# Probabilities turned as halves of 64 queries, and a new order of the pairs' work, in a fused attention and mixture-of-experts kernel

## The chip, the cores and the metric

One core of one Trainium2 chip runs the whole kernel. The metric is device time in microseconds. The core's engines run each its own program in order and meet through semaphores: PE (TensorE, matmuls; PEld are its loads of the stationary operand), DVE (VectorE), ACT (ScalarE), POOL (GpSimd) and SP, which issues the transfers.

## What is computed

Attention over 8 batches, 8 heads, 576 positions and 64 dimensions, with a causal mask by blocks of 64; then a top-1 mixture of 8 experts, where each expert keeps at most 80 tokens.

```python
scores = scale * np.matmul(q, k.transpose(0, 1, 3, 2))
mask = block_i >= block_j                      # blocks of 64
scores = np.where(mask, scores, -1000000000.0)
attn = np.exp(scores - np.max(scores, axis=-1, keepdims=True))
attn = attn / (np.sum(attn, axis=-1, keepdims=True) + 1e-09)
x = np.matmul(attn, v)                         # then tokens x 512
...
expert_idx = np.argmax(x @ w_gate, axis=1)     # 80 tokens kept for each expert
h = np.maximum(x[tok_idx] @ w1[e], 0.0)
out[tok_idx] = gate_w[tok_idx, None] * (h @ w2[e])
```

## The kernel before

Attention goes by pairs: two heads of one batch, 32 pairs in all, four to a batch. The 576 queries of a pair are five groups: u = 0 to 3 with 128 queries for each head, and group 4, the last 64 queries of both heads together (head 0 in partitions 0 to 63, head 1 in 64 to 127). Group u sees 128(u+1) keys.

For each group: `scores` multiplies q and k into PSUM (`sc`, two buffers of two banks; the two heads lie in the upper and lower 64 rows of the array and write to a bank each), with a small matmul of `mneg` and `mrow` that masks; `max` on DVE takes the negated row maximum; `soft` on ACT writes the exponentials to the probability tiles `P` in SBUF and sums them. Groups 2 and 0 share one score buffer ("20"). The probabilities then have queries on partitions, and the product with v needs keys there, so `back` turns them on PE, block by block, against the identity, into PSUM tiles `pm` (four buffers of one bank, line 252), and `take` copies each full bank to the SBUF tile `PT`: on ACT ("a") or DVE ("v") as `TAKE` says. `values` multiplies with v: half 0 is the 512 queries of groups 0 to 3, half 1 the 64 of group 4. `flip` on DVE turns the result into rows of tokens.

`TURN` is the order of one iteration, written by hand: an entry is a pair's offset from the iteration's number and what is done for that pair. The loop (line 552) walks it once an iteration, and every engine gets its instructions in the order in which the entries stand. So iteration i does scores and exponentials of pair i, the blocks of group 4 and `values` of pair i-1, loads (`load`, `load_v`) for later pairs and their turning on DVE (`prep`; POOL scales the queries). Three entries "step" an iteration take the next piece of a finished batch from a list: sums, store, logits, gate and so on, nine pieces for a batch, so three of four iterations have such steps, and one, called quiet here, has none. After the pairs follow the choice of tokens and the experts.

Before the change `back` knows seven kinds, each into one bank: "30" and "31" (group 3 of each head, four blocks of 128x128), "1", "2", "20" (group 0's block and group 2's last one, both heads), "4" (four blocks of group 4) and "44" (its fifth block, padded to 128 keys). That is 25 transpositions for a pair. "44" shares its bank with `values` half 1.

Of the kernel before, what the change touches and what calls it, by code (L numbers as in the profile page):

```python
# [7 lines left out]
F32 = mybir.dt.float32  # L8
# [10 lines left out]
P = 128  # L19
BLK = 64  # L20
NT = 5
# [3 lines left out]
CHUNK = 80  # L25


TAKE = {"back": {"30": "v", "31": "a", "1": "a", "2": "a", "20": "a", "4": "v", "44": "a"}, "values": {0: "a", 1: "a"}}

GROUPS = {"3": ((3, 0),), "20": ((2, 0), (0, 384)), "1": ((1, 0),)}  # L30

TURN = (
    (3, "load"),
    (2, "load_v"),
    (0, "begin"),
    (0, "scores", "3"),
    (0, "scores", "20"),
    (0, "max", "3"),
    (-1, "back", "44"),
    (-1, "back", "4"),  # L40
    (-1, "take", "back", "44"),
    (0, "max", "20"),
    (-1, "take", "back", "4"),
    (-1, "values", 0),
    (0, "soft", 3, 1),
    (0, "soft", 3, 0),
    (0, "soft", 2, 0),
    (0, "soft", 2, 1),
    (-1, "values", 1),
    (1, "prep", 1),  # L50
    (0, "soft", 0, 1),
    (0, "step"),
    (0, "soft", 0, 0),
    (-1, "take", "values", 1),
    (-1, "take", "values", 0),
    (0, "scores", "1"),
    (0, "max", "1"),
    (0, "step"),
    (0, "soft", 1, 0),
    (0, "soft", 1, 1),  # L60
    (0, "back", "30"),
    (0, "back", "31"),
    (1, "prep", 0),
    (0, "take", "back", "30"),
    (0, "scores_4"),
    (0, "max_4"),
    (0, "step"),
    (0, "back", "20"),
    (0, "back", "2"),
    (0, "take", "back", "31"),  # L70
    (-2, "flip"),
    (0, "back", "1"),
    (0, "soft_4"),
    (0, "take", "back", "1"),
    (0, "take", "back", "20"),
    (0, "take", "back", "2"),
)


# [1 line left out]
def tile_attn_moe(ctx, tc, q, k, v, w_gate, w1, w2, capacity, out, xs=None, dbg=None):  # L81
    nc = tc.nc
    B, H, S, D = q.shape
    NTOK, DM = out.shape
    E, _, F = w1.shape
# [24 lines left out]
    big = att2.enter_context(tc.tile_pool(name="big", bufs=2))  # L110
# [13 lines left out]
    for i in range(4):  # L124
        r = slice(32 * i, 32 * i + 32)
# [112 lines left out]
                    mybir.DependencyClass.Sync, mybir.DependencyReason.DATA))  # L238


    Pt = []
    for i in range(2):
        row = [pb.tile([P, 2, P * (t + 1)], F32, name=f"P{i}_{t}") for t in range(NT - 1)]
        Pt.append(row + [pb.tile([P, P * NT], F32, name=f"P{i}_4")])

    VT = [pb.tile([P, 2, D], F32, name=f"vt{i}") for i in range(4)]

# [125 lines left out]
    class Pair:  # L373


        def __init__(self, i):
            self.i = i
            self.b, self.pr = divmod(i, NP)
            self.h0 = 2 * self.pr
            self.out = {}  # L380
            self.T = {}

        def load(self):

            b, h0 = self.b, self.h0
            self.nat = [ld.tile([P, S // 32, 32], F32, name=f"ld{x}") for x in range(2)]
            for x in range(2):
                for h in range(2):
                    for i in range(2):
                        r = slice(h * D + 32 * i, h * D + 32 * i + 32)  # L390
                        nc.sync.dma_start(self.nat[x][r], (q, k)[x][b, h0 + h, :, 32 * i:32 * i + 32]
                                          .rearrange("(g r) d -> r g d", r=32))
# [68 lines left out]
        def back(self, x):  # L461


            if x == "30":
                self.PT = big.tile([P, 2, 13, P], F32, name="PT")
            PT = self.PT
            row = Pt[self.i % 2]
            pt = ps_m.tile([P, 512], F32, name="pm")
            if x in ("30", "31"):
                h = int(x[1])  # L470
                blocks = [(3, h, j) for j in range(4)]
                dst = PT[:, h, 3:13:3]
            elif x in ("1", "2"):
                u = int(x)
                blocks = [(u, h, j) for h in range(2) for j in range(2)]
                dst = PT[:, :, u:u + 4:3]
            elif x == "20":
                blocks = [b for h in range(2) for b in ((0, h, 0), (2, h, 2))]
                dst = PT[:, :, 0:9:8]
            else:  # L480
                blocks = [(4, None, j) for j in (range(4) if x == "4" else (4,))]
                dst = PT[:, :, 10:12] if x == "4" else PT[:, 0, 7]
            for n_, (u, h, j) in enumerate(blocks):
                src = row[u] if h is None else row[u][:, h]
                nc.tensor.transpose(pt[:, P * n_:P * (n_ + 1)], src[:, P * j:P * (j + 1)], ident)  # L485
            src = pt[:, 0:P * len(blocks)]
            if len(dst.shape) == 3:
                src = src.rearrange("p (j c) -> p j c", c=P)
            elif len(dst.shape) == 4:
                src = src.rearrange("p (h j c) -> p h j c", h=2, c=P)  # L490
            self.out["back", x] = (dst, src)
            if x == "44":
                self.shared = pt

        def values(self, half):

            av = ps_m.tile([P, 512], F32, name="pm") if half == 0 else self.shared[:, P:2 * P]
            PT = self.PT
            for j in range(4 + half):
                for h in range(2):  # L500
                    lhs = self.vt[:, h, :] if j == 4 else self.vn[:, h, j, :]
                    if half == 0:
                        rhs, c0, end = PT[:, h].rearrange("p b c -> p (b c)")[:, 512 * j:512 + 384 * j], P * j, 512
                    else:
                        b = PT[:, 0, 7] if j == 4 else PT[:, j // 2, 10 + j % 2]
                        rhs, c0, end = b[:, h * BLK:(h + 1) * BLK], 0, BLK
                    nc.tensor.matmul(av[h * D:(h + 1) * D, c0:end], lhsT=lhs, rhs=rhs,  # L507
                                     start=(j == 0), stop=(j == 3 + half))
            self.out["values", half] = ((self.bt.xT[:, self.pr, 0:512], av) if half == 0 else
                                        (self.bt.xT[:, self.pr, 512:S], av[:, 0:BLK]))  # L510

        def flip(self):
            self.bt.flip(self.pr)
# [1 line left out]
        def take(self, what, x):  # L515

            if TAKE[what][x] == "a":
                nc.scalar.copy(*self.out.pop((what, x)))  # L518
# [14 lines left out]
    n = B * NP  # L533
    pairs = [Pair(i) for i in range(n)]

    for row in Pt:
        nc.gpsimd.memset(row[4][:, S:], 0.0)
    for t_ in VT:
        nc.gpsimd.memset(t_[BLK:P], 0.0)
    nc.gpsimd.memset(wgd, 0.0)  # L540
# [57 lines left out]
    ps_m = ctx.enter_context(tc.tile_pool(name="ps_m2", bufs=3, **ps))  # L598
# [43 lines left out]
    for h in (1, 0):  # L642
        pl = pall[h]
        for k in range(2):
            for g in range(2):
# [3 lines left out]
                                          rhs=spread[:, k, g].rearrange("p j i -> p (j i)"),  # L649
                                          start=(k == 0 and g == 0), stop=(k == 1 and g == 1))  # L650
# [241 lines left out]
    with tc.For_i(0, again, 1):  # L892
# [24 lines left out]
        step = 1.0  # L917
        for it in range(28):
# [12 lines left out]
                         start=True, stop=True)  # L931
# [54 lines left out]
        with tc.For_i(0, more, 1):  # L986
# [24 lines left out]
            for e in range(E):  # L1011
# [67 lines left out]
```

## Time and profile before

| | us |
|---|---|
| median of 3 runs | 481.56 (481.30 to 481.87) |
| the profiled execution | 480.64 |
| its span | 478.4 |
| attention, from the first maximum to the choice of tokens | about 11 to 355 |
| experts, the rest of the span | about 123 |

The page gives busy time of each engine as a share of the whole span, so attention and experts are mixed in it. The groups by line show what one instruction takes (mean, ns) and what ended the idle time ahead of it. The order of time shows starts, and from start to next start is what a run of work really holds its engine: matmuls overlap, and a matmul's recorded length holds its way through the array too. Line 485 is the transpositions, 423, 430 and 439 the scores, 507 the values, 518 and 520 the copies of `take` on ACT and DVE, 444 and 448 the maxima, 452 and 457 the exponentials. These are the groups of the transpositions' PE side and of the value matmuls:

```profile
L485 PE MATMUL pm<-ident,P 128*128 128x128 f32 x800 | 108.7, 280 | 0.3 <-ACT P L457 0.2
L485 PEld LDWEIGHTS pm<-ident,P 128*128 128x128 f32 x800 | 87.1, 141 | 21.8 <-issue 15.9
L507 PE MATMUL pm<-PT,vn 128*64 128x64 f32 (+4 forms) x1024 | 91.1, 330 | 1.4 <-DVE PT L520 1.0
```

In such a row, 128*128 are the rows and columns of the stationary operand (here the probabilities) and 128x128 the moving one (here the identity).

### The profile page before, as it was taken

Reading aid. Unit: us, or ns where it says so; the run is one execution under the profiler, and the core shown is the slowest. Engines: PE = TensorE matmul, PEld = TensorE weight load, DVE = VectorE, ACT = ScalarE, POOL = GpSimd, SP = SyncE. Lnnn points to the kernel's source line nnn. Section 1 sums busy time; section 2 is a strip of 40 time slices with the busy share of each in tenths; the row PEclk is TensorE's granted clock in tenths of the full one; section 3 lists DMA queues with packets and bytes.
Section 4 is the critical chain, followed back from the end, with each engine's and each line's share of the span. In section 5 each row is a group of like instructions: output and inputs, shape, how many; then the busy total and the mean of one; then the engine's idle time right before and its main releaser. Section 6 shows DMA issues by size and latency. Waiting matters only on the chain. (4 is left out here: it accounts for less than half of the span.)

```text
span 478.4 us, 13557 instructions
## 1 busy us (share of the span) xinstructions
PE 442.0 (92%) x5403; PEld 309.5 (65%) x5403; DVE 283.9 (59%) x564; ACT 272.7 (57%) x863; POOL 54.0 (11%) x112
## 2 busy tenths in 40 slices
PE   5999999999999999999999999999984897889992
PEld 3566656666666666666666666666563887778981
DVE  3657767787696778769677876977672311011111
ACT  1787777787778778777877877787611110011100
POOL 1002120010010001001000100100024400000010
PEclk9799999999999999999999999999997699999997
DMA  7677746897887688887878877843259999995001
GB/s 120 115 138 143 163 84 118 175 272 141 173 172 149 123 184 241 152 180 150 168 138 182 226 138 157 174 108 77 70 107 336 308 395 398 394 394 215 18 19 30
DMA packets 230676, 84.29 MB, mean 176 GB/s; under 512 B 196877, under 2 KB 215309, under 8 KB 230608
## 3 DMA queue, kind: packets, MB, share of 16 engines
q1 hardware_dynamic: 229584, 80.93, 69.3%
q0 software_dynamic: 1024, 2.43, 1.7%
q8 instruction: 44, 0.72, 0.6%
q14 instruction: 24, 0.20, 0.1%
HBM read 63.21 MB, written 20.33 MB: 175 GB/s over the span
## 5 line engine op out<-in xcount | busy, mean ns | idle before, releaser
L452 ACT ACTIVATE P<-sc,negm 128x512 f32<-128x512 f32 (+3 forms) x256 | 132.2, 536 | 29.9 <-DVE negm L444 29.8
L444 DVE TENSOR_REDUCE negm<-sc 128x2 f32<-128x1024 f32 (+3 forms) x128 | 99.6, 820 | 73.9 <-PE sc L430 73.9
L485 PE MATMUL pm<-ident,P 128*128 128x128 f32 x800 | 108.7, 280 | 0.3 <-ACT P L457 0.2
L485 PEld LDWEIGHTS pm<-ident,P 128*128 128x128 f32 x800 | 87.1, 141 | 21.8 <-issue 15.9
L423 PE MATMUL sc<-T,T 64*128 64x128 f32 (+3 forms) x512 | 91.2, 471 | 3.5 <-POOL T L408 2.5
L507 PE MATMUL pm<-PT,vn 128*64 128x64 f32 (+4 forms) x1024 | 91.1, 330 | 1.4 <-DVE PT L520 1.0
L518 ACT COPY PT<-pm 128x512 f32<-128x512 f32 (+1 forms) x160 | 77.1, 530 | 23.2 <-PE pm L485 22.6
L507 PEld LDWEIGHTS pm<-PT,vn 128*64 128x64 f32 x1024 | 52.1, 137 | 41.4 <-issue 29.7
L423 PEld LDWEIGHTS sc<-T,T 64*128 64x128 f32 x512 | 41.9, 188 | 32.7 <-ACT PT L518 10.2
L452 ACT ACTIVATION_READ_ACCUMULATOR P<-sc,negm 128x1 f32 x256 | 54.4, 212 | 0.0
L405 DVE STREAM_TRANSPOSE T<-ld 128x576 f32<-128x576 f32 x64 | 49.1, 768 | 4.1 <-DMA ld<-in_k_dram 4.1
L408 POOL TENSOR_SCALAR T<-T 128x576 f32<-128x576 f32 x32 | 21.5, 673 | 246.6 <-DVE T L405 181.6
L824 PE MATMUL ps<-xsT,w 128*64 128x80 f32 x1024 | 41.6, 243 | 4.2 <-issue 4.2
L824 PEld LDWEIGHTS ps<-xsT,w 128*64 128x64 f32 x1024 | 39.4, 144 | 5.6 <-issue 5.0
L520 DVE COPY PT<-pm 128x512 f32<-128x512 f32 x64 | 42.7, 667 | 0.5 <-PE pm L485 0.5
L824 PE MATMUL av<-hT,w 128*64 128x80 f32 x1024 | 38.2, 234 | 4.4 <-issue 4.4
L824 PEld LDWEIGHTS av<-hT,w 128*64 128x64 f32 x1024 | 36.4, 137 | 6.3 <-issue 6.3
L439 PE MATMUL sc<-T,T 64*64 64x288 f32 x256 | 38.5, 419 | 0.0
L457 ACT ACTIVATE P<-sc,negm 128x576 f32<-128x576 f32 x32 | 23.8, 745 | 20.3 <-DVE negm L448 20.3
L844 ACT ACTIVATE hT<-ps 128x320 f32<-128x320 f32 x16 | 7.0, 437 | 49.1 <-PE ps L824 49.1
L448 DVE TENSOR_REDUCE negm<-sc 128x1 f32<-128x576 f32 x32 | 24.3, 758 | 8.6 <-PE sc L439 7.8
L852 DVE COPY yT<-av 128x320 f32<-128x320 f32 x8 | 3.9, 492 | 38.1 <-PE av L824 38.1
(158 smaller groups left out, 303.2 us busy)
## 6 DMA issues: line engine op xcount, KB each, us to landing
w<-in_moe_w_dram SPq DMA_DIRECT2D x16, 2048.0 KB, 20.3
ld<-in_q_dram SPq DMA_DIRECT2D x128, 72.0 KB, 3.0
ld<-in_k_dram SPq DMA_DIRECT2D x128, 72.0 KB, 2.7
out_dram<-zero SPq DMA_DIRECT2D x18, 512.0 KB, 4.6
xs<-Y SPq DMA_DIRECT2D x32, 288.0 KB, 4.4
vn<-in_v_dram SPq DMA_DIRECT2D x64, 128.0 KB, 2.8
vt<-in_v_dram SPq DMA_DIRECT2D x32, 32.0 KB, 2.4
xs<-rs SPq DMA_DIRECT2D x8, 16.0 KB, 2.4
```

Source lines behind the costliest of these rows:

```text
L405: nc.vector.transpose(t, self.nat[x].rearrange("p g d -> p (g d)"))
L423: nc.tensor.matmul(s[:, h, c:c + P * (u + 1)], lhsT=self.T[0][r, P * u:P * (u + 1)], rhs=self.T[1][r, 0:P * (u + 1)], start=(x == 0), stop ...
L439: nc.tensor.matmul(s[r, c, 0:288], lhsT=self.T[0][r, 512:S], rhs=self.T[1][r, 288 * c:288 * (c + 1)], start=True, stop=True)
L444: nc.vector.tensor_reduce(self.negm[:, u], self.s[g][:, :, c:c + P * (u + 1)], axis=AX.X, op=ALU.max, negate=True)
L448: nc.vector.tensor_reduce(self.negm[:, 4, 0:1], self.s["4"][:, :, 0:288], axis=AX.XY, op=ALU.max, negate=True)
L452: nc.scalar.activation(Pt[self.i % 2][u][:, h], self.s[g][:, h, c:c + P * (u + 1)], AF.Exp, bias=self.negm[:, u, h:h + 1], scale=1.0, accu ...
L457: nc.scalar.activation(Pt[self.i % 2][4][:, 0:S].rearrange("p (c k) -> p c k", c=2), self.s["4"][:, :, 0:288], AF.Exp, bias=self.negm[:, 4 ...
L485: nc.tensor.transpose(pt[:, P * n_:P * (n_ + 1)], src[:, P * j:P * (j + 1)], ident)
L507: nc.tensor.matmul(av[h * D:(h + 1) * D, c0:end], lhsT=lhs, rhs=rhs, start=(j == 0), stop=(j == 3 + half))
L518: nc.scalar.copy(*self.out.pop((what, x)))
L520: nc.vector.tensor_copy(*self.out.pop((what, x)))
L824: yield nc.tensor.matmul(dst(b)[64 * c:64 * (c + 1)], lhsT=w_[:, a, col:col + 64], rhs=x_[:, a], start=(a == 0), stop=(a == n - 1))
```

## The change

Turning: `back` now has three kinds of eight blocks, A (group 3, both heads), B (groups 1 and 2, first two blocks) and C (four blocks of group 4, and the blocks "20" had), and "44". Each block of A, B and C is turned as two halves of 64 queries: queries 0 to 63 into one bank, 64 to 127 into another, two `pm` tiles at a time, so 48 halves and one whole block for a pair. The identity is cut to the same half. "44" no longer pads its 64 keys.

SBUF: A and B go to `PT`, C to a new tile `PF`, both with the half as an outer index; the small tile `PL` holds "44". P1 and P3 have one buffer now in place of two. `values` half 0 reads both halves as one moving operand in runs of 64 columns, and goes in six steps of 128, 384, 384, 128, 128 and 128 columns in place of four of 512, 384, 256 and 128. Copies: A0, B0, C0, C1 and "44" on ACT, A1 and B1 on DVE.

```diff
-TAKE = {"back": {"30": "v", "31": "a", "1": "a", "2": "a", "20": "a", "4": "v", "44": "a"}, "values": {0: "a", 1: "a"}}
+TAKE = {"back": {"A0": "a", "A1": "v", "B0": "a", "B1": "v", "C0": "a", "C1": "a", "44": "a"},
+        "values": {0: "a", 1: "a"}}
...
+            pt = [ps_m.tile([P, 512], F32, name="pm") for _ in range(2)]
...
+            if x == "A":
+                blocks = [(3, h, j) for h in range(2) for j in range(4)]
+            elif x == "B":
+                blocks = [(u, h, j) for h in range(2) for j in range(2) for u in (1, 2)]
             else:
-                blocks = [(4, None, j) for j in (range(4) if x == "4" else (4,))]
...
+                blocks = [(4, None, j) for j in range(4)] + [b for h in range(2) for b in ((0, h, 0), (2, h, 2))]
             for n_, (u, h, j) in enumerate(blocks):
-                src = row[u] if h is None else row[u][:, h]
-                nc.tensor.transpose(pt[:, P * n_:P * (n_ + 1)], src[:, P * j:P * (j + 1)], ident)
...
+                from_ = row[u] if h is None else row[u][:, h]
+                for c in range(2):
+                    r = slice(c * BLK, (c + 1) * BLK)
+                    nc.tensor.transpose(pt[c][:, n_ * BLK:(n_ + 1) * BLK], from_[r, P * j:P * (j + 1)], ident[r, r])
...
+            steps = [(0, "X", 4, 0, P), (0, 0, 3, P, 512), (1, 3, 6, P, 512), (3, 11, 12, 3 * P, 512),
+                     (2, 8, 9, 3 * P, 512), (2, "X", 5, 2 * P, 3 * P)]
...
+                        rhs = (self.PF[:, :, 2 * h + b1:2 * h + b1 + 1] if b0 == "X" else self.PT[:, :, h, b0:b1])
+                        rhs = rhs.rearrange("p c b r -> p b c r")
```

The new order, engine by engine. On PE, from the scores "3" (512 columns) of one pair into the scores "20" (384 and 128); rows of line 430 (431 after) are the mask. Before:

```order
L423 MATMUL sc<-T_989,T_1024 128x512 x2
L430 LDWEIGHTS mrow
L430 MATMUL sc<-mneg,mrow 128x64
L430 LDWEIGHTS mrow
L430 MATMUL sc<-mneg,mrow 128x64
L423 MATMUL sc<-T_989,T_1024 128x384 x2
L423 MATMUL sc<-T_989,T_1024 128x128 x2
```

After:

```order
L424 MATMUL sc<-T_1530,T_1430 128x512 x2
L431 LDWEIGHTS mrow
L431 MATMUL sc<-mneg,mrow 128x64
L431 LDWEIGHTS mrow
L431 MATMUL sc<-mneg,mrow 128x64
L489 MATMUL pm<-ident,P_0_129 128x64 x8
L489 MATMUL pm<-ident,P_0_123 128x64 x2
L489 MATMUL pm<-ident,P_0_126 128x64 x2
L489 MATMUL pm<-ident,P_0_123 128x64 x2
L489 MATMUL pm<-ident,P_0_126 128x64 x2
L424 MATMUL sc<-T_1530,T_1430 128x384 x2
```

C, the sixteen halves of the pair before (P_0_129 is group 4), now stands between the two; before, group 4 was turned behind both.

On PE, from group 3's transpositions (P_3_126 before, P_0_128 after) over the scores of group 4 (288 columns). Before:

```order
L485 MATMUL pm<-ident,P_3_126 128x128 x8
L439 MATMUL sc<-T_1413,T_1438 64x288 x4
L290 MATMUL pm<-xT,wgd 32x384 x4
L485 MATMUL pm<-ident,P_0_123 128x128
L485 MATMUL pm<-ident,P_2_125 128x128
```

After:

```order
L489 MATMUL pm<-ident,P_0_128 128x64 x16
L519 MATMUL pm<-PF,vn 64x64 x8
L519 MATMUL pm<-pl_131,vt_133 64x64 x2
L440 MATMUL sc<-T_1530,T_1430 64x288 x4
L489 MATMUL pm<-ident,P_0_125 128x64 x2
L489 MATMUL pm<-ident,P_1_127 128x64 x2
```

Values half 1 of the pair before moved in ahead of group 4's scores, and B, groups 1 and 2 in turn, stands behind them (the row of line 290 is a batch step).

On ACT, around the exponentials of group 4 (576 columns). Before:

```order
L452 ACTIVATE P_1_129,sums<-sc,negm 128x256 x2
L518 COPY PT<-pm 128x4x128
L457 ACTIVATE P_4_132,sums_1759<-sc,negm 128x576
L518 COPY PT<-pm 128x2x2x128 x3
L518 COPY PT<-pm 128x128
L452 ACTIVATE P_3_126,sums<-sc,negm 128x512 x2
```

After:

```order
L453 ACTIVATE P_0_125,sums<-sc,negm 128x256 x2
L529 COPY xT<-pm 128x64
L529 COPY PT<-pm 128x8x64
L458 ACTIVATE P_1_130,sums_1427<-sc,negm 128x576
L529 COPY PT<-pm 128x2x2x128
L529 COPY PF<-pm 128x512 x2
```

One copy (B0) and the two of C now follow the exponentials of group 4; the copy of "44" went further down, behind exponentials of groups 2 and 0.

More of the change, by code (lines that the diff above doesn't have):

```diff
@@ L33 @@
     (3, "load"),
+    (0, "begin"),
+    (1, "prep", 0),
+    (0, "scores", "3"),
+    (-1, "back", "C"),
+    (0, "scores", "20"),
+    (-1, "take", "back", "C0"),
+    (-1, "take", "back", "C1"),
     (2, "load_v"),
-    (0, "begin"),
-    (0, "scores", "3"),
-    (0, "scores", "20"),
     (0, "max", "3"),
[L39 to L44, printed above, removed]
     (0, "soft", 3, 1),
     (0, "soft", 3, 0),
+    (0, "max", "20"),
+    (0, "step"),
+    (-1, "back", "44"),
+    (-1, "values", 0),
+    (0, "soft", 0, 0),
+    (0, "scores", "1"),
+    (0, "soft", 2, 1),
+    (0, "back", "A"),
+    (1, "prep", 1),
+    (-1, "take", "back", "44"),
     (0, "soft", 2, 0),
-    (0, "soft", 2, 1),
-    (-1, "values", 1),
-    (1, "prep", 1),
+    (0, "max", "1"),
+    (0, "take", "back", "A1"),
     (0, "soft", 0, 1),
-    (0, "step"),
-    (0, "soft", 0, 0),
-    (-1, "take", "values", 1),
     (-1, "take", "values", 0),
-    (0, "scores", "1"),
-    (0, "max", "1"),
-    (0, "step"),
     (0, "soft", 1, 0),
     (0, "soft", 1, 1),
[L61 to L64, printed above, removed]
+    (-1, "values", 1),
     (0, "scores_4"),
+    (0, "back", "B"),
+    (-1, "take", "values", 1),
+    (-2, "flip"),
     (0, "max_4"),
+    (0, "take", "back", "B1"),
+    (0, "take", "back", "A0"),
     (0, "step"),
[L68 to L72, printed above, removed]
     (0, "soft_4"),
-    (0, "take", "back", "1"),
-    (0, "take", "back", "20"),
-    (0, "take", "back", "2"),
+    (0, "take", "back", "B0"),
+    (0, "step"),
 )
@@ L238, in weights @@
                     mybir.DependencyClass.Sync, mybir.DependencyReason.DATA))
[L241 to L244, printed above, removed]
+    P0, P1, P2, P3 = [[pb.tile([P, 2, P * (t + 1)], F32, name=f"P{t}_{i}") for i in range(1 + (t in (0, 2)))]
+                      for t in range(NT - 1)]
+    Pt = [[x[i % len(x)] for x in (P0, P1, P2, P3)] + [pb.tile([P, S], F32, name=f"P4_{i}")] for i in range(2)]
+    PL = [pb.tile([P, P], F32, name=f"pl{i}") for i in range(2)]
     VT = [pb.tile([P, 2, D], F32, name=f"vt{i}") for i in range(4)]
@@ L381, in __init__ @@
             self.T = {}
+            self.PT = None
         def load(self):
@@ L461, in back @@
         def back(self, x):
-            if x == "30":
-                self.PT = big.tile([P, 2, 13, P], F32, name="PT")
-            PT = self.PT
             row = Pt[self.i % 2]
[L468 to L479, printed above, removed]
-            else:
-                blocks = [(4, None, j) for j in (range(4) if x == "4" else (4,))]
-                dst = PT[:, :, 10:12] if x == "4" else PT[:, 0, 7]
+            if x == "44":
+                dst = PL[self.i % 2][0:BLK]
+                self.last = ps_m.tile([P, 512], F32, name="pm")
+                src = self.last[0:BLK, 0:P]
+                nc.tensor.transpose(src, row[4][:, 512:S], ident)
+                self.out["back", x] = (dst, src)
+                return
@@ new lines, in back @@
+            pt = [ps_m.tile([P, 512], F32, name="pm") for _ in range(2)]
+            if x in "AB" and self.PT is None:
+                self.PT = big.tile([P, 2, 2, 12, BLK], F32, name="PT")
+            if x == "A":
+                blocks = [(3, h, j) for h in range(2) for j in range(4)]
+            elif x == "B":
+                blocks = [(u, h, j) for h in range(2) for j in range(2) for u in (1, 2)]
+            else:
+                self.PF = big.tile([P, 2, 8, BLK], F32, name="PF")
+                blocks = [(4, None, j) for j in range(4)] + [b for h in range(2) for b in ((0, h, 0), (2, h, 2))]
@@ L483, in back @@
             for n_, (u, h, j) in enumerate(blocks):
-                src = row[u] if h is None else row[u][:, h]
[L485 to L491, printed above, removed]
@@ L492, in back @@
-            if x == "44":
-                self.shared = pt
-        def values(self, half):
-            av = ps_m.tile([P, 512], F32, name="pm") if half == 0 else self.shared[:, P:2 * P]
-            PT = self.PT
-            for j in range(4 + half):
+                from_ = row[u] if h is None else row[u][:, h]
+                for c in range(2):
+                    r = slice(c * BLK, (c + 1) * BLK)
+                    nc.tensor.transpose(pt[c][:, n_ * BLK:(n_ + 1) * BLK], from_[r, P * j:P * (j + 1)], ident[r, r])
@@ new lines, in back @@
+            for c in range(2):
+                src = pt[c]
+                if x == "A":
+                    dst = self.PT[:, c, :, 2:12:3]
+                    src = src.rearrange("p (h j r) -> p h j r", h=2, j=4)
+                elif x == "B":
+                    dst = self.PT[:, c, :, 0:6].rearrange("p h (j u) r -> p h j (u r)", j=2)[:, :, :, 0:P]
+                    src = src.rearrange("p (h j r) -> p h j r", h=2, j=2)
+                else:
+                    dst = self.PF[:, c].rearrange("p b r -> p (b r)")
+                self.out["back", f"{x}{c}"] = (dst, src)
@@ L500, in values @@
+        def values(self, half):
+            av = ps_m.tile([P, 512], F32, name="pm") if half == 0 else self.last[:, P:P + BLK]
+            steps = [(0, "X", 4, 0, P), (0, 0, 3, P, 512), (1, 3, 6, P, 512), (3, 11, 12, 3 * P, 512),
+                     (2, 8, 9, 3 * P, 512), (2, "X", 5, 2 * P, 3 * P)]
+            if half == 1:
+                steps = [(j, None, j, 0, BLK) for j in range(5)]
+            for n_, (j, b0, b1, c0, end) in enumerate(steps):
                 for h in range(2):
                     lhs = self.vt[:, h, :] if j == 4 else self.vn[:, h, j, :]
-                    if half == 0:
-                        rhs, c0, end = PT[:, h].rearrange("p b c -> p (b c)")[:, 512 * j:512 + 384 * j], P * j, 512
-                    else:
-                        b = PT[:, 0, 7] if j == 4 else PT[:, j // 2, 10 + j % 2]
-                        rhs, c0, end = b[:, h * BLK:(h + 1) * BLK], 0, BLK
@@ L507, in values @@
-                    nc.tensor.matmul(av[h * D:(h + 1) * D, c0:end], lhsT=lhs, rhs=rhs,
-                                     start=(j == 0), stop=(j == 3 + half))
+                    to = av[h * D:(h + 1) * D, c0:end]
+                    if half == 1:
+                        rhs = PL[self.i % 2][:, h * BLK:(h + 1) * BLK] if j == 4 else self.PF[:, h, j]
+                    else:
+                        rhs = (self.PF[:, :, 2 * h + b1:2 * h + b1 + 1] if b0 == "X" else self.PT[:, :, h, b0:b1])
+                        rhs = rhs.rearrange("p c b r -> p b c r")
+                        to = to.rearrange("p (b c r) -> p b c r", c=2, r=BLK)
@@ L509, in values @@
+                    nc.tensor.matmul(to, lhsT=lhs, rhs=rhs, start=(n_ == 0), stop=(n_ == len(steps) - 1))
             self.out["values", half] = ((self.bt.xT[:, self.pr, 0:512], av) if half == 0 else
-                                        (self.bt.xT[:, self.pr, 512:S], av[:, 0:BLK]))
+                                        (self.bt.xT[:, self.pr, 512:S], av))
         def flip(self):
@@ L534, in tile_attn_moe @@
     pairs = [Pair(i) for i in range(n)]
-    for row in Pt:
-        nc.gpsimd.memset(row[4][:, S:], 0.0)
+    for t_ in PL:
+        nc.gpsimd.memset(t_[BLK:P], 0.0)
     for t_ in VT:
```

## Prediction

> **What bounds the kernel now.** I read the page's busy times first, then busy time by stretch, then TensorE's order of time through one iteration. On the page:
>
> ```profile
> span 478.4 us, 13557 instructions
> PE 442.0 (92%) x5403; PEld 309.5 (65%) x5403; DVE 283.9 (59%) x564; ACT 272.7 (57%) x863; POOL 54.0 (11%) x112
> ```
>
> The share is a mean over two stages, so here is attention alone: busy time by stretch (columns: length, then busy time of PE, PEld, DVE, ACT, POOL with counts, clock, DMA share, GB/s). The first row is four iterations (one batch, four pairs of heads), the second one quiet iteration, without batch steps.
>
> ```profile
> 207.10:248.90 41.80, 41.80 (x403) 26.69 (x401) 31.88 (x57) 32.33 (x104) 3.59 (x6) 1.00 0.79 160
> 102.46:112.39 9.93, 9.93 (x92) 6.40 (x91) 7.00 (x10) 7.64 (x24) 0.67 (x1) 1.00 0.83 167
> ```
>
> PE is busy without a gap, at the full clock; ACT (7.64 of 9.93 us) and DVE (7.00) are not. An iteration is 41.80/4 = 10.45 us on average and 9.93 when quiet, so batch steps cost 0.52. But pipelined matmuls can be "busy" while they wait, so I checked start times. TensorE's order of time in the quiet iteration (start, length, operation):
>
> ```profile
> 102.46 1.13 PE L423 MATMUL sc<-T,T 64*128 64x512 f32 x4
> ...
> 103.45 1.12 PE L423 MATMUL sc<-T,T 64*128 64x384 f32 x8
> ...
> 104.55 0.77 PE L485 MATMUL pm<-ident,P 128*128 128x128 f32 x5
> 105.25 2.84 PE L507 MATMUL pm<-PT,vn 128*64 128x512 f32 x32
> 107.91 0.29 PE L507 MATMUL pm<-PT,vt 128*64 128x64 f32 x4
> 108.13 0.70 PE L423 MATMUL sc<-T,T 64*128 64x256 f32 x4
> ...
> 108.79 1.09 PE L485 MATMUL pm<-ident,P 128*128 128x128 f32 x8
> 109.81 1.19 PE L439 MATMUL sc<-T,T 64*64 64x288 f32 x8
> 110.93 1.53 PE L485 MATMUL pm<-ident,P 128*128 128x128 f32 x12
> 112.39 1.13 PE L423 MATMUL sc<-T,T 64*128 64x512 f32 x4
> ```
>
> From start to next start: scores "3" 0.99, scores "20" 1.10, five transpositions 0.70, both values 2.88, scores "1" 0.66, eight transpositions 1.02, scores_4 1.12, twelve transpositions 1.46: sum 9.93. These eight numbers are the attention's clock. Of the transpositions, twelve against eight give (1.46-1.02)/4 = 0.110 each, and 1.02-8x0.110 = 0.14 is left per run: the cost of entering a run of another tile shape, about 0.06 of it a first load (rows below), the rest, as I read it, an array run empty. There are seven such changes of shape in the iteration.
>
> **The transpositions (gain).** 24 of the 25 blocks of a pair become two halves of 64 rows and 64 moving columns, one in the upper and one in the lower rows of the array, with a bank each. What does such a couple of halves cost? Nothing in the trace is a half transposition, so I take neighbours: the order of time in narrow stretches, and the mean of one form.
>
> ```profile
> 107.69 0.40 PE L507 MATMUL pm<-PT,vn 128*64 128x64 f32 x7
> 108.45 0.38 PE L423 MATMUL sc<-T,T 64*128 64x256 f32 x2
> L423 PE MATMUL sc<-T,T 64*128 64x256 f32 x100 | 17.6, 428 | 0.0
> 108.79 0.14 PEld L485 LDWEIGHTS pm<-ident,P 128*128 128x128 f32 x1 [0.24 <-issue]
> 108.79 0.20 PEld L485 LDWEIGHTS pm<-ident,P 128*128 128x128 f32 x2 [0.24 <-issue]
> ```
>
> Matmuls of 64 moving columns, two side by side in column halves, go from 107.69 to 107.91 in four couples: about 0.058 us a couple (0.055 to 0.06 by the rounding). That the row halves work side by side too is seen in the scores: two matmuls of the two heads, upper and lower rows, different banks, take 0.38 us together, where one alone lasts 0.428 on average. And a load of 128 stationary columns fits in 0.058: of the first two loads of a run, the second adds 0.06 (0.20-0.14). So the couple costs between 0.058 (as the neighbour) and 0.110 (as a whole block today) if the halves run together; I take 0.058, since its two ingredients each have a row. Gain: 24 x (0.110-0.058) = 1.25 us per iteration.
>
> The Trainium skill ("TensorE: Matmul & The Clock Gate", section "LDWEIGHTS (loading the stationary operand)") speaks against this: a load's time goes by its columns, about columns/1.2 ns, and not by its rows. Both halves keep 128 columns, so by the page a couple would wait about 107 ns for loads (an estimate from the page), and the sum would be that of the second rival below. The two load rows above disagree: 128 columns in about 60 ns.
>
> **The order (gain).** Row halves of 64x128 are also the shape of the scores. The new order puts C between scores "3" and "20", A behind scores "1", and B ahead of the next scores "3", so these stand without a change of shape; five changes are left of seven. New run, start to start: scores "3" 0.99, C 8x0.058 = 0.46, scores "20" 1.10, block 44 0.11, values 0 (2.88 less values 1 of ten couples at 0.058, so 2.30; two more steps add 0.02) 2.32, scores "1" 0.66-0.09 = 0.57, A 0.46+0.14 = 0.60, values 1 0.58+0.14 = 0.72, scores_4 1.12, B 0.46. Sum 8.45, against 9.93.
>
> **A wait takes the place of work.** C needs the whole of soft_4, which hangs on max_4 and scores_4:
>
> ```profile
> 104.92 0.27 ACT L518 COPY PT<-pm 128x128 f32<-128x128 f32 x1 [0.79 <-PE pm L485]
> 111.05 0.76 DVE L448 TENSOR_REDUCE negm<-sc 128x1 f32<-128x576 f32 x1 [0.20 <-PE sc L439]
> 111.84 0.74 ACT L457 ACTIVATE P<-sc,negm 128x576 f32<-128x576 f32 x1 [0.66 <-DVE negm L448]
> 112.48 0.19 ACT L457 ACTIVATION_READ_ACCUMULATOR P<-sc,negm 128x1 f32 x1
> ```
>
> From the start of scores_4 (109.81) to the end of that chain (112.67) are 2.86 us; PE starts 0.05 after an ACT copy (104.92+0.27 to 105.25, with rounding), and the first load is 0.06: C begins 2.97 after scores_4. PE has 1.12 + B 0.46 + scores "3" 0.99 = 2.57 of work for that time, so it waits 0.40 in each iteration. Before, block 4 stood behind scores "20", 1.12+1.46+0.99+1.10 = 4.67 us after scores_4, so the same chain was covered. Behind C queue scores "20", values and everything else on PE, so nothing hides it. Quiet period: 8.45+0.40 = 8.85.
>
> **What costs nothing.** Evictions stay six full copies, four on ACT and two on DVE, plus the small one. Their targets lie in runs of 64 columns. Rows of strided and of plain targets are alike, 595 and 606 ns:
>
> ```profile
> L518 ACT COPY PT<-pm 128x512 f32<-128x512 f32 x128 | 68.7, 595 | 0.6
> L518 ACT COPY xT<-pm 128x512 f32<-128x512 f32 x32 | 19.4, 606 | 0.0
> ```
>
> Values 0 now reads its moving operand in runs of 64. If each run cost as much as an instruction of its own, it would be 40 couples at 0.058 = 2.32 against 2.30-0.14 = 2.16 today: up to 0.16 an iteration, 5 us in all, or nothing. I take nothing, as instructions of 128 and more columns are what is issued, and keep 5 us for the range. P1 and P3 have one buffer instead of two; their readers (B, A) run half an iteration ahead of the next writer, and ACT's 7.64 us leave 1.2 free in 8.85. The scaling on POOL (0.67 us in the quiet iteration) starts earlier, and SP's queue keeps its order (q, k, then v). The batch steps stay three an iteration at 0.52: some break up runs of one shape (four more changes at 0.14 a batch, 4 us in all), some fill the 0.40 wait (three of four iterations, 9 us in all); I keep 0.52, and both for the range. The experts' stage is untouched.
>
> **Sum.** 10.45 - (8.85+0.52) = 1.08 an iteration; between the first and the last of 32 pairs lie 31 iterations: 33.5 us. The profiled execution took 480.64 (span 478.4 and 2.2 around it), so 447.1; the median shown, 481.56, is 0.9 above it: 448.0.
>
> **Rivals.** (1) Cross-engine waits cost more: with DVE and ACT near 8 us of 9.4 (31.88/4 and 32.33/4), a copy or maximum that comes late makes PE wait a second time. One more wait like that at C, 0.40 x 31, gives 460. Chance 0.15. (2) The 128 stationary columns and not the moving ones set the pace: couples at 0.110. PE's sum is then 8.45+24x0.052 = 9.70, the wait at C is covered (1.12+0.87+0.99 = 2.98), and 9.70+0.52 gives 0.23 an iteration: 474. The load rows speak against it. Chance 0.07. (3) Transfers become the bound: a share of 0.79 of 41.80 us is 33 us of work for a batch, 8.3 an iteration; it fits in 9.37 only if the queues reach a share of 0.88. At 0.85 as a ceiling, 9.7 an iteration, the gain is 0.75 x 31: 458. Against it: in the list of waits DVE waited for a load of q or k once, at the start (total, times, longest):
>
> ```profile
> DVE T L405 <- DMA ld<-in_k_dram: 4.1, 1, 4.1
> ```
>
> Chance 0.10. (4) **Slower:** the halves run one after another. At 0.058 a half, a couple is 0.116: PE's sum is 9.84, plus 0.52 is 10.36, 479; at 0.110 a half (load not hidden) a couple is 0.220: 12.34, plus 0.52 is 12.86, and (12.86-10.45) x 31 gives 556. It turns slower from 0.060 a half. Against it stand the two scores matmuls in 0.38. Chance 0.07, most of it slower.
>
> **Numbers.** The forecast has 0.61, from 440 (the wait filled by batch steps, 9 us) to 453 (runs of 64, 5 us). Rivals 1 and 3 reach to 460; a couple at 0.075 instead of 0.058 adds 12.6 us, 461; so the range is 440 to 464, and leaves out rivals 2 and 4. A measurement of this kernel can tell about 0.2% from no change. Faster by more 0.93, within 0.01, slower by more 0.06.
>
> **What would show it.** Right: 1,568 transpositions in place of 800, the couples every 0.058 us; a quiet iteration of 8.85; PE idle about 0.4 us ahead of C, put down to ACT's soft_4; DMA share up to 0.88; the experts' stage as long as before. Wrong: couples at 0.11 or halves one by one; PE waiting at B or at values 0 for copies; DVE waiting for loads; a changed step cost in the batch.

## The result and the profile after

| | before | after |
|---|---|---|
| median, us | 481.72 (481.30 to 482.03) | 463.78 (462.94 to 464.77, 4 runs) |
| ratio, with its 95% interval | | 0.9628 (0.9611 to 0.9645) |
| span of the profiled execution, us | 478.4 | 460.7 |

The kernel is 17.9 us faster where 33.5 were forecast. The page of the changed kernel:

```profile
span 460.7 us, 15580 instructions
PE 415.8 (90%) x6427; PEld 294.5 (64%) x6427; DVE 284.1 (62%) x564; ACT 271.8 (59%) x863; POOL 54.1 (12%) x112
...
L489 PE MATMUL pm<-ident,P 64*128 64x64 f32 x1536 | 70.0, 231 | 1.7 <-DVE prod L308 0.4
```

PE lost 26 us of busy time, more than the span lost: some of what was won became idle time. Where, is seen in the stretches (columns as before): a quiet iteration, four iterations early on, and 41 us late in attention.

```profile
97.17:106.18 9.01, 8.87 (x127) 5.74 (x123) 7.19 (x11) 7.83 (x26) 0.67 (x1) 1.00 0.87 170
97.60:135.40 37.80, 37.66 (x533) 24.30 (x531) 31.74 (x58) 32.08 (x103) 3.59 (x6) 1.00 0.80 164
249.00:290.00 41.00, 34.89 (x457) 22.17 (x455) 26.71 (x43) 27.10 (x86) 2.80 (x5) 0.92 0.82 178
```

Early on four iterations take 37.80 us in place of 41.80, a mean of 9.45. Late, PE stands 6.1 of 41 us, and the granted clock is 0.92. So there are two questions: is the regular iteration as forecast, and what stalls the others?

The regular one first. TensorE's order of time in the quiet iteration (start, length, operation):

```profile
97.17 0.71 PE L489 MATMUL pm<-ident,P 64*128 64x64 f32 x16
97.71 1.08 PE L424 MATMUL sc<-T,T 64*128 64x384 f32 x8
...
98.78 0.30 PE L472 MATMUL pm<-ident,P 128*64 128x128 f32 x1
99.04 0.44 PE L519 MATMUL pm<-PF,vn 128*64 128x128 f32 x4
...
101.35 0.70 PE L424 MATMUL sc<-T,T 64*128 64x256 f32 x4
...
101.92 0.69 PE L489 MATMUL pm<-ident,P 64*128 64x64 f32 x16
102.54 0.69 PE L519 MATMUL pm<-PF,vn 128*64 128x64 f32 x16
...
103.27 1.19 PE L440 MATMUL sc<-T,T 64*64 64x288 f32 x8
104.39 0.71 PE L489 MATMUL pm<-ident,P 64*128 64x64 f32 x16
104.94 1.08 PE L424 MATMUL sc<-T,T 64*128 64x512 f32 x4
...
106.18 0.40 PE L489 MATMUL pm<-ident,P 64*128 64x64 f32 x6
```

From start to start, against the forecast's terms:

| run | forecast | measured |
|---|---|---|
| C | 0.46 | 0.54 |
| scores "20" | 1.10 | 1.07 |
| block 44 | 0.11 | 0.26 |
| values 0 | 2.32 | 2.31 |
| scores "1" | 0.57 | 0.57 |
| A | 0.60 | 0.62 |
| values 1 | 0.72 | 0.73 |
| scores_4 | 1.12 | 1.12 |
| B | 0.46 | 0.55 |
| scores "3" and the wait at C | 0.99 + 0.40 | 1.24 |
| sum | 8.85 | 9.01 |

The lengths of all iterations follow from the starts of the first maximum (VectorE's 128x1024 reduction). Before, a batch of four took 10.22, 9.94, 10.72 and 10.92 us (mean 10.45); after, a regular one 8.65, 8.91, 9.56 and 10.76 (mean 9.47, forecast 9.37). But iterations 17, 20, 24, 25 and 26 last 10.67, 11.06, 11.2, 13.66 and 10.85, and iteration 4 lasts 12.18 (before, 11.78). The list of waits of the changed kernel (total, times, longest) has what stands behind them:

```profile
DVE T L406 <- DMA ld<-in_q_dram: 15.1, 6, 5.6
...
PEld pm L489 <- ACT P L458: 9.7, 18, 0.7
...
DVE iota_c L212 <- POOL iota_c L210: 1.9, 1, 1.9
```

The first is new: before, VectorE waited for such a load once, at the start; here two of the six waits fall at the start, the other four in iterations 18 to 26. The second is the forecast wait at C. The third belongs to iteration 4 (see the constants below). Here is the longest stall, in the order of time of SP's queue, of VectorE and of PE (in square brackets the idle time ahead of an instruction, and what ended it):

```profile
254.39 0.59 SPq L233 DMA_DIRECT2D w<-in_moe_w_dram  x1
255.08 8.93 SPq L392 DMA_DIRECT2D ld<-in_q_dram  x4
264.10 2.59 SPq L392 DMA_DIRECT2D ld<-in_k_dram  x4
...
266.75 0.78 DVE L406 STREAM_TRANSPOSE T<-ld 128x576 f32<-128x576 f32 x1 [5.61 <-DMA ld<-in_q_dram]
...
270.23 1.22 PE L424 MATMUL sc<-T,T 64*128 64x256 f32 x4 [4.53 <-ACT P L453]
```

A weight load of 2 MB for the experts is issued at 254.39. Behind it four loads of q take SP 8.93 us to issue, where four of k take 2.59; VectorE waits 5.61 us for q; and as a pair's q is turned on VectorE ahead of a maximum of the pair before, the maximum, the exponentials and PE's scores "1" wait too. PE stands 4.53 us.

Such bulk work on SP's queue is of two kinds: three weight loads (iterations 8, 16 and 24), and 18 transfers of 512 KB that fill the output with zeros (`clear`, `out_dram<-zero`) in iterations 4 to 31. The change touches neither.

### The profile page after: what moved, and what is told of

Read it like the earlier page. It is cut to its first block, busy times and chain, and to the rows that moved or that the text cites. A ratio compares the mean times of both kernels' runs of the same rounds, so it can differ in the third digit from the quotient of the medians.

```text
span 460.7 us, 15580 instructions
## 1 busy us (share of the span) xinstructions
PE 415.8 (90%) x6427; PEld 294.5 (64%) x6427; DVE 284.1 (62%) x564; ACT 271.8 (59%) x863; POOL 54.1 (12%) x112
## 5 line engine op out<-in xcount | busy, mean ns | idle before, releaser
L453 ACT ACTIVATE P<-sc,negm 128x128 f32<-128x128 f32 (+3 forms) x256 | 133.3, 531 | 32.0 <-DVE negm L445 30.1
L424 PE MATMUL sc<-T,T 64*128 64x128 f32 (+3 forms) x512 | 96.1, 475 | 11.6 <-ACT P L453 10.7
L489 PEld LDWEIGHTS pm<-ident,P 64*128 64x128 f32 x1536 | 57.6, 142 | 33.9 <-ACT P L458 9.7
L489 PE MATMUL pm<-ident,P 64*128 64x64 f32 x1536 | 70.0, 231 | 1.7 <-DVE prod L308 0.4
L424 PEld LDWEIGHTS sc<-T,T 64*128 64x128 f32 x512 | 43.2, 193 | 33.5 <-ACT P L453 14.1
L519 PE MATMUL pm<-PT,vn 128*64 128x128 f32 (+1 forms) x512 | 60.7, 379 | 0.0
L406 DVE STREAM_TRANSPOSE T<-ld 128x576 f32<-128x576 f32 x64 | 48.8, 763 | 16.5 <-DMA ld<-in_q_dram 15.1
L519 PE MATMUL pm<-PF,vn 128*64 128x64 f32 (+1 forms) x768 | 48.7, 249 | 0.9 <-ACT PF L529 0.9
L519 PEld LDWEIGHTS pm<-PT,vn 128*64 128x64 f32 x512 | 33.5, 137 | 22.9 <-issue 22.9
L529 ACT COPY PF<-pm 128x512 f32<-128x512 f32 x64 | 34.4, 589 | 15.5 <-PE pm L489 15.5
L529 ACT COPY PT<-pm 128x512 f32<-128x512 f32 x64 | 37.8, 591 | 0.0
L519 PEld LDWEIGHTS pm<-PF,vn 128*64 128x64 f32 x768 | 32.4, 139 | 7.5 <-ACT PF L529 1.1
```

The costliest lines, as they stand in the source:

```text
L406: nc.vector.transpose(t, self.nat[x].rearrange("p g d -> p (g d)"))
L424: nc.tensor.matmul(s[:, h, c:c + P * (u + 1)], lhsT=self.T[0][r, P * u:P * (u + 1)], rhs=self.T[1][r, 0:P * (u + 1)], start=(x == 0), stop ...
L453: nc.scalar.activation(Pt[self.i % 2][u][:, h], self.s[g][:, h, c:c + P * (u + 1)], AF.Exp, bias=self.negm[:, u, h:h + 1], scale=1.0, accu ...
L489: nc.tensor.transpose(pt[c][:, n_ * BLK:(n_ + 1) * BLK], from_[r, P * j:P * (j + 1)], ident[r, r])
L519: nc.tensor.matmul(to, lhsT=lhs, rhs=rhs, start=(n_ == 0), stop=(n_ == len(steps) - 1))
```

## The experiments

Each ratio is to the kernel before, run on the same chip beside the experiment (medians 481.36 to 481.86).

### The transfers: without the clearing, and the kernel before without it

```diff
-            if i >= 4 and (i % 2 or i % 8 == 4) and i < n:
-                clear(cleared)
-                cleared += 1
...
-        while cleared < nz:
-            clear(cleared)
-            cleared += 1
```

> The changed kernel without the 18 transfers of 0.5 MB that clear the output (the clearing is left out). Theory T (late transfers: the queue of loads cannot follow the shorter iterations, q arrives late, PE waits): the long iterations around 184, 203 and 214 us fall to the usual four lengths 8.65, 8.9, 9.6, 10.8, those around the third weight load (243 to 278 us) stay longer, and the time falls by 4 to 8 us, to 456 to 460. Rival D (DVE and ACT come late by themselves, late loads are only a symptom): within 1.5 us of the changed kernel's 463.8.

Measured: 451.86 us, ratio 0.9389 (0.9359 to 0.9418); this kernel leaves the output uncleared. All stalls are gone, also those behind weight loads; the gain was 4 us more than the theory gave. From iteration 8 on every batch takes the regular 37.9 us. The same cut in the kernel before:

> The kernel before without the clearing (left out). Theory T: no change (480.6 to 481.9), since its longer iterations leave the queue time and DVE waited for no load. If transfers disturb matmuls or copies in some other way, at any speed of the loop, it gets faster by as much as the changed kernel does.

Measured: 481.79 us, ratio 1.0002 (0.9983 to 1.0020). So the clearing cost nothing at the old pace and 11.9 us (463.78 - 451.86) at the new one.

The slow issue behind a weight load is not new, and it costs nothing by itself. Here are the four loads of q behind the third weight load in the kernel before, then in the changed kernel without the clearing; VectorE waits for neither:

```profile
259.54 8.43 SPq L391 DMA_DIRECT2D ld<-in_q_dram  x4
...
243.04 8.24 SPq L392 DMA_DIRECT2D ld<-in_q_dram  x4
```

What differs is the lead. By the trace these four loads (pair 27) landed 15.5 us before VectorE was free to turn them in the kernel before, 2.6 us before it without the clearing, and 5.4 us after it in the changed kernel. Part of the lead seems to have gone with the new order, which turns q at the start of an iteration: in the run with the halves in series below, near the old pace and with every transfer in its old place, the lead is 6.5 us. Shorter iterations and the two bulk streams used up the rest.

### The same transfers, moved

All 18 clearing transfers at the end of attention, six in each of the last three iterations:

```diff
-            if i >= 4 and (i % 2 or i % 8 == 4) and i < n:
+            for _ in range(6 * (n - 3 <= i < n)):
                 clear(cleared)
```

> The changed kernel with all 18 clearing transfers issued in the last three pairs' iterations (six each), when no q, k and v are left to load. Theory T: as without the clearing, 456 to 460, if the 9.4 MB fit into the lull at the end of attention; 1 to 4 us more if they delay the last store and the experts' weights. Rival D: 463.8 or more.

Measured: 452.82 us, ratio 0.9402 (0.9371 to 0.9433). The output is cleared here as in the changed kernel, and the gain is the same as without the clearing, within the measurement. Instead, only the three weight loads moved:

```diff
-            if i in range(n // 4, n // 4 + 8 * FW0, 8):
+            if i in range(n - 3, n - 3 + FW0):
                 weights(1)
```

> The changed kernel with the three early weight loads of 2 MB moved from iterations 8, 16 and 24 to the last three pairs; clearing as in the changed kernel. If clearing and weights only hurt together, the stretch from 243 to 278 us loses its stall of about 8 us, the two small ones near 184 and 203 us partly stay, and the experts' stage may start later: 455 to 462. If clearing alone makes the queue late, the stalls stay and the time is 463 or more.

Measured: 451.92 us, ratio 0.9396 (0.9379 to 0.9412), again all of it, where the theory gave a part. VectorE's wait for q in this kernel, in its list of waits:

```profile
DVE T L406 <- DMA ld<-in_q_dram: 3.1, 2, 1.7
```

Both waits are at the start. Either bulk stream alone leaves q a lead (pair 27: 5.6 us with late clearing, 9.9 us with late weights); both together do not. It is not the share of busy transfer engines alone that decides: with the clearing late, four iterations that hold a weight load run with the regular length at a share of 0.81 (first row, stretches of that kernel), while the changed kernel stalls in a stretch with a mean of 0.82 and has a quiet iteration without a stall at 0.87 (both shown above).

```profile
155.40:193.30 37.90, 37.76 (x534) 24.43 (x529) 31.84 (x58) 32.18 (x104) 3.59 (x6) 1.00 0.81 172
```

### The same transfers, issued by ScalarE

Is it SP's order or the transfers themselves? The clearing in its old places, on ScalarE's queue:

```diff
-                nc.sync.dma_start(ov[i], zero.rearrange("p (r d) -> p r d", r=2))
+                nc.scalar.dma_start(ov[i], zero.rearrange("p (r d) -> p r d", r=2))
```

> The changed kernel with the 18 clearing transfers at their old places in the program, but issued from ACT's queue and not from SP's. If SP's queue is what falls behind (a load stands behind a clearing transfer that is slow to issue), the time is that of the kernel that clears late, 452 to 454, plus up to 1 for ACT's issuing. If the transfer engines themselves are too full in those stretches, loads are late from either queue: 459 to 464.

Measured: 502.89 us, ratio 1.0453 (1.0436 to 1.0471), outside of what either theory gave. The order of time on ScalarE shows why (ACTq is its issuing):

```profile
131.48 0.49 ACT L292 COPY lgT<-pm 128x384 f32<-128x384 f32 x1
134.95 0.37 ACTq L150 DMA_DIRECT2D out_dram<-zero  x1
135.37 1.07 ACT L529 COPY PF<-pm 128x512 f32<-128x512 f32 x2 [3.40 <-DMA xs<-Y]
```

ScalarE stands for 3.40 us around an issue that itself takes 0.37, and C's copies come late; PE waits for those copies 40.1 us in all. In this kernel's list of waits:

```profile
PEld pm L519 <- ACT PF L529: 40.1, 14, 6.7
```

What ended the stand was the landing of a store that SP had begun to issue 6.6 us earlier:

```profile
128.31 2.86 SPq L280 DMA_DIRECT2D xs<-Y  x2
```

This is a wait for a semaphore. In the trace the transfers of SP and ScalarE take eight completion semaphores in turn, and an issue first waits until the transfer that last had its semaphore has landed. ScalarE's issue at 134.95 had the semaphore of that store, which landed at 134.93; at least twelve of its 18 issues waited in this way, for a store of xs or a load of q. So the run shows what such a shared semaphore costs on an engine that computes. It leaves open whether SP's order or the load on the transfer engines makes q late: VectorE waited for q only at the start, but the kernel was also 8% slower than the changed one.

The Trainium skill ("DMA: Bandwidth & Descriptors", section "Issuing engines are not separate DMA queues") says that transfers of all issuers share the same engines, and that a second issuer only saves issue time. Nothing here speaks against it: the 3.40 us are the wait for the semaphore, and the issue itself took 0.37. That the engines are shared, no run here isolates.

### The halves: one bank after the other

The loop over the two halves outside that over the blocks, so that a run goes through all upper halves, then all lower ones:

```diff
-            for n_, (u, h, j) in enumerate(blocks):
-                from_ = row[u] if h is None else row[u][:, h]
-                for c in range(2):
+            for c in range(2):
+                for n_, (u, h, j) in enumerate(blocks):
```

> The changed kernel with the halves issued bank by bank: all eight upper halves first, then all eight lower ones, so that neighbours in PE's program share rows of the array. If the gain is from halves that work side by side, a half now costs 0.058 alone, the couples 0.116, a quiet iteration 9.8 to 10.2 and the time 478 to 484. If a half is cheap by itself, whatever stands beside it, nothing changes: 463.8 within 1.5.

Measured: 475.15 us, ratio 0.9874 (0.9848 to 0.9901); quiet iterations 9.88 to 9.89, and no stalls at this pace. Against the stall-free kernel (452.8) the neighbourhood of the halves is worth 22.3 us, more than the whole gain of the change. The rows of TensorE, around B and at A:

```profile
109.16 0.83 PE L489 MATMUL pm<-ident,P 64*128 64x64 f32 x13
109.77 0.69 PE L424 MATMUL sc<-T,T 64*128 64x512 f32 x1
109.83 0.35 PE L489 MATMUL pm<-ident,P 64*128 64x64 f32 x3
110.02 1.07 PE L424 MATMUL sc<-T,T 64*128 64x512 f32 x3
...
115.98 0.99 PE L489 MATMUL pm<-ident,P 64*128 64x64 f32 x16
116.90 0.69 PE L519 MATMUL pm<-PF,vn 128*64 128x64 f32 x16
```

A takes 0.92 us in place of 0.62 (start to start). At B the last three halves run beside the next scores, which have begun in the other rows of the array; even so the iteration is 0.98 longer than the regular quiet one (9.89 - 8.91).

### The order around C

These two stand on the kernel with late clearing. First, C behind scores "20" instead of ahead of them:

```diff
     (0, "scores", "3"),
-    (-1, "back", "C"),
     (0, "scores", "20"),
+    (-1, "back", "C"),
```

> The late-clearing kernel with C moved behind the scores 20. The wait for soft_4 ahead of C is then covered (1.10 us more of work before C), with no more changes of shape, but the two copies of C on ACT now stand openly between C and values 0: about 1.2 us (PE to ACT 0.2, 0.59 and 0.47, less block 44's 0.11). By the chain of the prediction a quiet iteration goes from 8.9 to 9.6 to 9.9 and the time to 470 to 480. If PE's own work alone set the pace, it would fall by 0.4 an iteration, to 441.

Measured: 476.56 us, ratio 0.9909 (0.9890 to 0.9927), quiet iterations 9.98. The wait at C is covered there, but C's copies end later, and the values wait for them. In its list of waits:

```profile
PEld pm L519 <- ACT PF L529: 32.4, 32, 1.1
```

Second, scores_4 ahead of values 1, so that 0.73 us more of work cover the chain to C:

```diff
-    (-1, "values", 1),
     (0, "scores_4"),
+    (-1, "values", 1),
     (0, "back", "B"),
```

> The late-clearing kernel with scores_4 issued ahead of values 1, so that values 1 (0.72 us) stands beside max_4 and soft_4 and the wait at C (0.40) is covered. If that wait is the only thing above PE's own 8.45, a quiet iteration falls to 8.5 and the time by 8 to 12 us, to 441 to 445. If another loop lies right under it (score buffers that ACT frees late, copies that values 0 waits for), PE waits elsewhere and the time stays at 452 to 455.

Measured: 457.86 us, ratio 0.9511 (0.9494 to 0.9529), 5.0 us slower than without the move. PE no longer waits at C in the quiet iteration (rows of TensorE):

```profile
97.19 1.13 PE L424 MATMUL sc<-T,T 64*128 64x512 f32 x4
...
98.18 0.69 PE L489 MATMUL pm<-ident,P 64*128 64x64 f32 x16
```

C comes 0.99 us after scores "3", as forecast for a covered chain; yet quiet iterations last 9.01 between maxima, and the batch 38.19 instead of 37.88. Of the 4.7 us between the two profiled spans, 2.6 lie between the first and the last maximum, 1.6 behind the last and the rest ahead of the first. Another loop seems to lie right under the wait. One row of the list of waits is new, ScalarE waiting for values 1, which now come behind scores_4 (with late clearing alone: 2.0 us, once):

```profile
ACT xT L529 <- PE pm L519: 22.6, 32, 3.9
```

That this is the loop was not isolated.

### ScalarE's copies of C

On the kernel with late weights: C0's copy on VectorE, because block 44 took 0.26 us instead of 0.11 until values 0 began.

```diff
-"C0": "a", "C1": "a"
+"C0": "v", "C1": "a"
```

> The kernel with late weights (451.9), with the copy of C's upper halves taken by VectorE instead of ScalarE. Theory that ScalarE, with both copies of C and block 44's, is what values 0 waits for (0.15 us an iteration): the wait goes, quiet 8.76 to 8.85, 447 to 449.5. Rival: VectorE takes the first maximum 0.7 us later, and with it the exponentials and scores 1; then values 0 is earlier but scores 1 waits, and the kernel is as fast or slower: quiet 8.9 to 9.5, 452 to 468.

Measured: 457.48 us, ratio 0.9493 (0.9467 to 0.9518), quiet iterations 9.04: the rival. The copy stands ahead of the maxima on VectorE, and ScalarE's wait for them grows to 55.2 us (17.7 in the kernel with late weights). Order of time on VectorE, then the row from the list of waits:

```profile
108.38 0.69 DVE L531 COPY PF<-pm 128x512 f32<-128x512 f32 x1 [0.36 <-PE pm L489]
108.99 2.41 DVE L445 TENSOR_REDUCE negm<-sc 128x2 f32<-128x1024 f32 x3
```

```profile
ACT P L453 <- DVE negm L445: 55.2, 34, 9.6
```

The premise fails too. C1's copy on ScalarE, block 44 and values 0 in the same iteration:

```profile
108.41 0.59 ACT L529 COPY PF<-pm 128x512 f32<-128x512 f32 x1 [0.35 <-PE pm L489]
109.25 0.30 PE L472 MATMUL pm<-ident,P 128*64 128x128 f32 x1
109.48 0.44 PE L519 MATMUL pm<-PF,vn 128*64 128x128 f32 x4
```

Both copies have ended by 109.07, 0.41 us before values 0, and block 44 still takes 0.23 until they begin. So of its 0.26 in the changed kernel at most 0.03 was a wait for C's copies.

### The constants

What makes iteration 4 so long? The wait was there before (1.9 us, once), but iteration 4 is now 2.71 above the mean of its kernel, before 1.33. In the kernel with late weights, VectorE's order of time there:

```profile
58.12 0.18 DVE L212 TENSOR_TENSOR iota_c<-sameR,iota_c 128x16 f32<-128x16 f32 x1 [1.95 <-POOL iota_c L210]
```

The router's constants are made there; VectorE waits for GpSimd, and the maxima stand behind it. The edit issues GpSimd's part behind the scaling of the next pair, and VectorE's four instructions that need it one iteration later (`constants3` holds them):

```diff
-            if i == 5:
-                constants2()
...
+                if (i, what, *args) == (5, "prep", 0):
+                    constants2()
+                if (i, what, *args) == (6, "prep", 0):
+                    constants3()
```

> The changed kernel with the three weight loads at the end of attention (as in the run with late weights, 451.9) and with the router's constants split: GpSimd's part is issued behind the scaling for the next pair, and VectorE's four small instructions that need GpSimd's iota stand one iteration later, so that VectorE never waits for GpSimd (it waited 1.95 us there). Theory: in the iteration of 12.2 us VectorE's wait delays the first maximum, ACT's exponentials and so scores 1 (PE stood 1.98 us); it falls to 9.0 to 9.6, and the kernel takes 448.5 to 449.8. Rival: that iteration is long because of something else of the pipeline's start (loads, the weights' gap); then it stays above 11 and the time at 451.5 to 452.5.

Measured: 449.65 us (447.90 to 451.45), ratio 0.9334 (0.9294 to 0.9375). The iteration falls from 12.18 to 10.32, not to 9.6, and the kernel gains 2.3 us; a smaller wait of VectorE for GpSimd is left:

```profile
57.21 0.37 DVE L197 TENSOR_REDUCE sameR<-ident 128x16 f32<-128x128 f32 x1 [0.78 <-POOL sameR L196]
```

By its median this is the fastest kernel of the study; its interval ends just short of that of the kernel with late weights (from 0.9379). The same with the clearing late as well:

> As the run before, and the 18 clearing transfers at the end of attention too. Theory: clears and weight loads only hurt together, so moving the second of them as well brings nothing: within 1 us of the run before (448 to 450). Rival: six clears an iteration beside the late weight loads pile up at the end of attention, and the last iterations and the experts' first weights come late: 452 to 456.

Measured: 455.57 us, ratio 0.9465 (0.9436 to 0.9495): the rival. Attention is as long as in the run before (291.0 and 291.9 us from the first maximum to the last), but clearing and weights now meet the last tokens on their way out. How many, KB each, and the median time from issue to landing, from 295 to 330 us, in this kernel and in the one before it:

```profile
xs<-Y SPq DMA_DIRECT2D x8, 288.0 KB, 9.8
```

```profile
xs<-Y SPq DMA_DIRECT2D x8, 288.0 KB, 6.5
```

From the last maximum to the end are 149.9 us in place of 145.1. Moving both streams to the end was too much here; spreading them was not tried.

## Why the prediction was right, and where its size came out wrong

**The gain by halves: right in kind, a little too large.** The terms with no transpositions in them stand within 0.03 us. Couples run side by side; C, between two scores with no change of shape, takes 0.54/8 = 0.068 a couple, where 0.058 was taken, so C and B came out 0.08 and 0.09 too long, and A 0.02. Rival 2 (0.110 a couple) and rival 4 (one by one) are out; what halves in series cost was measured, a quiet iteration of 9.89 (rival 4 had 9.84 for PE).

The Trainium skill ("TensorE: Matmul & The Clock Gate", section "LDWEIGHTS (loading the stationary operand)") makes the load's time go by its columns, about 107 ns for 128; sixteen such loads one after another would take 1.7 us, eight side by side in couples 0.86, both estimates from the page. TensorE's loads of C show 0.57 us for sixteen, so the measurement decides against it for these halves:

```profile
97.16 0.57 PEld L489 LDWEIGHTS pm<-ident,P 64*128 64x128 f32 x16 [0.36 <-ACT P L458]
```

**The wait at C: right in place, somewhat too large.** Its row stands in the list of waits, and scores "3" with the wait are 1.24 where 1.39 was forecast. Covering it (scores_4 early) made the kernel slower: something else then sets 9.01 a quiet iteration, close above 8.91.

**Block 44: the miss that offsets it.** It took 0.26 where 0.11 was taken. The forecast had found 0.14 for each run of another tile shape and put none on this lone block; 0.11 + 0.14 is 0.25. It is hardly a wait for C's copies, as the run with C0 on VectorE shows (0.23 with the copies long done). That the rest is the change of shape fits the forecast's own figure, but no run isolates it. The 0.09 taken off scores "1" names no row either; that run came out at 0.57, as forecast.

**Values in runs of 64: free, as taken.** Values 0 took 2.31, forecast 2.32.

**The batch steps: nearly right.** They cost 9.47 - 8.91 = 0.56, forecast 0.52. With the quiet iteration at 8.91 the regular mean is 0.10 over the forecast: 3.1 us over 31 iterations.

**The transfers: the mis-sized term.** "SP's queue keeps its order" stood under what costs nothing, and rival 3 was worked out with a mean share of 0.79 and a ceiling. That looked at the mean of one batch; what decides is how early q lands in the worst one, and the shorter iterations, the earlier turn of q and the two bulk streams together took its lead from 15.5 us to nothing (pair 27). "DVE waiting for loads" was among the prediction's own signs of being wrong, and it came. Rival 3 so came true in part, beside the forecast and not in its place: the regular batches keep 9.47, others stall.

**The sum.** From the first maximum to the last the kernel before takes 322.5 us, the changed one 306.0: 16.5 of the 17.7 that the span lost. To the forecast's 33.5 are missing 17.0:

| | us |
|---|---|
| stalls behind bulk transfers (306.0 against 294.9 with late clearing) | 11.1 |
| regular mean 9.47 for 9.37, 31 times | 3.1 |
| the iteration with the constants: 2.71 above its mean, before 1.33 | 1.4 |
| not accounted for (first and last iterations among it) | 1.4 |

The first line was shown by taking either kind of bulk transfer away. Moving the constants won 2.3 us, more than the third line, so that line's size is only bounded. The second is read from the order of time and was not removed by any run.

**The range: luck.** The time of 463.78 lies 0.2 us inside the range's upper end. That end came from a second wait at C, from a ceiling on the mean share and from slower couples; loads that come late in single iterations, which filled most of the gap, had no price in it. That the time still fell inside was luck, not foresight.

## What to carry to other kernels

When a loop gets shorter, price the traffic of its worst iteration and not of its mean: transfers that cost nothing at the old pace (ratio 1.0002 without them) took over a third of the forecast gain at the new one (11.9 of 33.5 us), and moving one of the two bulk streams elsewhere gave it back. Watch how long before its use a load lands: that lead runs down before anything waits. A transfer moved to an engine that computes can bring a wait for another queue's semaphore with it. In this kernel halves of a stationary operand gained most when neighbours in the program alternated between the halves of the array (22.3 us). Where two or three engines' loops are within a few tenths of a microsecond, filling one visible wait moves the bound and can lose time, so try it before counting it.

## What the runs showed of the hardware that was not expected

- SP's issues grow long behind a bulk transfer: behind a weight load of 2 MB four loads of q took 8.93 us to issue in the changed kernel, 8.43 in the kernel before and 8.24 without the clearing, where the four loads of k behind them took 2.59 in the changed one. That an issue is held until transfers ahead have moved on is a reading; no run isolates it.
- ScalarE stood 3.40 us ahead of copies for an issue of 0.37 us, because the issue waited for the semaphore of a store that SP had issued.
- With halves in series, matmuls of two different runs overlap when they use different rows of the array: B's last three halves ran while the next scores had already begun.
- In the stretch with the stalls the granted clock was 0.92, against 1.00 in regular ones. From 270.2 to 273.5, right behind the 4.53 us of idle time, it was 0.50, and the four matmuls of scores "1" span 1.22 us there, in place of 0.70.
